# Two runs of eighteen W_out products instead of four runs of nine in the second MLP layer of an attention-and-MLP kernel

## The chip, the cores and the metric

The kernel runs on one core of one Trainium2 chip. The metric is the device time of one execution in microseconds (us). The kernel before takes 757.12 us, the median of three runs that lie between 756.71 and 757.83 us.

## What is computed

A clustered attention over two batches of 768 tokens with eight heads is followed by two MLP layers over all 1536 tokens (512 features, 2048 hidden features). Only the second MLP layer is touched by the change:

```python
def _moe2_ref(x, w_in, w_out):
    h = x @ w_in
    r = np.maximum(h, 0.0)
    g = r * r
    return (g @ w_out).astype(np.float32)
```

The first layer has the same shape with another activation. The weights come in as 64-bit floats, viewed as pairs of 32-bit words, and the kernel turns each 128-row or 128-column chunk into 32-bit floats on the way ("decode").

## The kernel before, in words

The two layers are worked off in 32 slots, numbered 0 to 31 here: layer, then batch, then a pair of hidden chunks (256 hidden features). Slots 16 to 23 are the second layer's first batch, slots 24 to 31 its second batch. A slot computes the hidden values of its pair (`h`, 256 features by 768 tokens) and applies the activation. The product with W_out belongs to the slot before: `second` returns a list `pend` of four closures, and each is a quarter of the W_out products of the previous slot, which are issued in between.

Every fp32 operand is held as a high and a low part (both fp32r), so each product is three matmuls: high by high, low by high, high by low.

From slot 8 on, the hidden values are formed from seven block products instead of eight, which accumulate in two PSUM banks, A and B. `product` issues 6 matmuls of 384 columns. Products 1, 3, 5 and 7 go to A, and products 2, 4 and 6 to B. Between them A and B are read while they hold partial sums: ScalarE copies A after product 1 and after product 3 and B after product 4 (lines 1123, 1139, 1142), and VectorE adds B after product 2, A after product 5 and B after product 6 (`total`). Product 7 is read by `active` (Relu on ScalarE, line 828). Product 5 accumulates in the bank that the copy after product 3 reads, and product 6 in the one that the copy after product 4 reads. The next slot swaps the banks, so its product 2 starts afresh in the bank that held product 7.

`active` squares twice on ScalarE, once rounded to fp32r (`gh`, line 831) and once in fp32 (line 832), and `low` subtracts the two on VectorE (`gl`, line 835). The left half of the first chunk (LO) is ready after product 2, the second chunk after product 6, and the right half of the first chunk (HI) after product 7.

In the second layer a quarter of `pend` is 9 matmuls of 512 columns (line 854): three token blocks by three terms. A slot has 36 of them and 42 matmuls in block products. The quarters stand behind products 2, 4, 6 and 7.

Work for later slots is spread over ScalarE and VectorE by hand. `early` and `late` split the next weights (lines 929 and 930: a cast on ScalarE, a subtraction on VectorE). `sums` forms weight sums on VectorE. `absolute` and `do` decode chunks for later: line 87 takes absolute values on ScalarE, lines 96, 98, 101 and 104 follow on VectorE one after the other, and step 4 stores a W_in chunk to DRAM or splits a W_out chunk (cast at line 110 on ScalarE, subtraction at 111 on VectorE). `COUNTS` gives two decode tasks to most slots, three to slot 17, one to slot 23, and none from slot 24 on. At a batch's end (`last`, slot 23) the five calls `nxt.part` split the next batch's inputs (cast at line 902, subtraction at 903); `rest`, the loop at line 1136, splits the last two in slots 16 and 24.

ScalarE, VectorE, TensorE and SyncE's DMA issues each stand in the order in which the code was written.

Of the kernel before, what the change touches and what calls it, by code (L numbers as in the profile page):

```python
# [35 lines left out]
def tile_kernel(ctx, tc, q, k, v, cent, w_in1, w_out1, w_in2, w_out2, cw_cols, out):  # L36
# [768 lines left out]
    LO, HI, ALL = slice(0, QB), slice(QB, S), slice(0, S)  # L805
# [9 lines left out]
    def total(layer, c, at, ps):  # L815

        dst = h[:, c, at]
        if layer == 0:
            nc.vector.tensor_tensor(out=dst, in0=ps, in1=dst, op=ALU.add)
        else:  # L820
            nc.vector._custom_dve(TENSOR_ADD_SAT, out=dst, in0=ps, in1=dst, s0=TOP, s1=0.0)  # L821
# [12 lines left out]
    def low(g, c, at):  # L834
        nc.vector.tensor_sub(g[1][:, at], h[:, c, at], f32(g[0][:, at]))  # L835
# [120 lines left out]
    def product(ps, w, wi, x, start=False):  # L956
        terms = [(0, 0), (0, 1), (1, 0)]
        for j, (a, z) in enumerate(terms):
            for kc in range(2):
                nc.tensor.matmul(ps, w[a][:, wi, kc * P:(kc + 1) * P], x[z][kc],  # L960
                                 start=start and j == kc == 0, stop=j == 2 and kc == 1, skip_group_check=True)
# [23 lines left out]
    def absolute():  # L985
        n = len(ready)
        if n < len(tasks) and n < len(fetched) and 5 * n <= len(steps) + 5:
            layer, kind, fc = tasks[n]
            if layer:
                if q < NP:  # L990
                    return
                t = rooms[n % 2]
            elif kind:
                t = room
                if 5 * n > len(steps) and tasks[n - 1][:2] != (0, 0):
                    return
            else:
                t = weights[fc // 2].chunk(fc)
            ready.append(magnitude(fetched[n], t.bitcast(U32)))
# [29 lines left out]
    slots = [(layer, b, p) for layer in range(2) for b in range(B) for p in range(NP)]  # L1029
    nxt = None  # L1030
    at_bank = 0
    ends = None
    for q, (layer, b, p) in enumerate(slots):
        bank = first if q == 0 else [
            duo.tile([P, QB], F32, tag=("sd", "pt0")[(at_bank + i) % 2], name="ps") for i in range(2)]
        A, B_ = bank
        n = COUNTS[q] if q < len(COUNTS) else 0
        more = q + 1 < len(slots)
        last = p == NP - 1 and more
        if p == 0:  # L1040
            combos = nxt
        if p == (3 if q >= NP else 1) and q < 3 * NP:
            nxt = Combos(slots[q + NP][1])
        wq = weights.get(q)
        ga, gb = g_tiles(), g_tiles()

        def before(k):
            if pend:
                pend[k]()
            if p == 0 and ends:  # L1050
                finish(*ends, k)

        def do(i, ks):
            if i < n:
                for k in ks:
                    step(k)

        if q + 2 < 2 * NP and q in PLAIN and q or q >= 2 * NP - 1 and more:
            at = q + 1 + (q in PLAIN)
            weights[at] = Weights(slots[at][0], slots[at][2], at >= NP)  # L1060
        wn = weights.get(q + 1)
        if q == 0:
            pend = None
            ends = None
            y = y_tiles()
            bank = [first, [hidden(xs, second_w, i, y[4 + i][:, 0:QB]) for i in range(2)]]
            for c, g in ((0, ga), (1, gb)):
                for i, at in enumerate((LO, HI)):
                    active(0, g, c, at, bank[c][i])
                if not c:  # L1070
                    absolute()
                for i, at in enumerate((LO, HI)):
                    low(g, c, at)
                if not c:
                    step(0)
                    step(1)
                    step(2)
                    step(3)
            wn.plain(1)
            step(4)  # L1080
            absolute()
            for k in range(4):
                step(k)
            absolute()
            step(4)
        elif q in PLAIN:
            extra = list(EXTRA.get(q, ()))
            for c, g in ((0, ga), (1, gb)):
                for i, at in enumerate((LO, HI)):
                    u = 2 * c + i  # L1090
                    bank[i] = hidden(xs, wq.sides[c], i, bank[i] if not c else None)
                    active(0, g, c, at, bank[i])
                    if u:
                        do(u - 1, (4,))
                    if i:
                        if q + 1 in PLAIN:
                            wn.plain(c)
                        else:
                            wn.early(c)
                    absolute()  # L1100
                    do(u, (0, 1))
                    low(g, c, at)
                    do(u, (2, 3))
                    if i:
                        before(2 * c)
                        before(2 * c + 1)
                    if i and not c and q + 1 not in PLAIN:
                        wn.sums()
                    if u == 3:
                        do(u, (4,))  # L1110
                    if extra:
                        kind, j = extra.pop(0)
                        (nxt.part if kind else nxt.sum)(j)
        else:
            at_bank = 1 - at_bank
            x = combos.tiles
            if p == 0:
                rooms = [t3_p.tile([P, S], F32, tag="t3", name="room")[:, 0:DM] for _ in range(2)]
            product(A, wq.x, wq.B11, x[Combos.A11], True)
            wq.late()  # L1120
            if q + 2 < 2 * NP:
                weights[q + 2] = Weights(slots[q + 2][0], slots[q + 2][2], q + 2 >= NP)
            nc.scalar.copy(h[:, 0, LO], A)
            if n:
                absolute()
            product(B_, wq.x, wq.B21, x[Combos.A12], True)
            total(layer, 0, LO, B_)
            active(layer, ga, 0, LO)
            do(0, (0, 1))
            if last:  # L1130
                nxt.part(0)
            do(0, (2, 3))
            low(ga, 0, LO)
            before(0)
            if p == 0:
                while len(x) < 7:
                    combos.part(len(x))
            product(A, wq.x, wq.T2, x[Combos.S2])
            nc.scalar.copy(h[:, 1, LO], A)
            do(0, (4,))  # L1140
            product(B_, wq.x, wq.T1, x[Combos.S1], True)
            nc.scalar.copy(h[:, 1, HI], B_)
            if more:
                wn.early(0)
            if last:
                nxt.part(1)
                nxt.part(2)
            if n > 1:
                absolute()
            before(1)  # L1150
            do(1, (0, 1))
            if n > 2:
                do(1, (2, 3))
            product(A, wq.y, wq.T3, x[Combos.S3])
            total(layer, 1, HI, A)
            product(B_, wq.y, wq.B22, x[Combos.S4])
            total(layer, 1, LO, B_)
            active(layer, gb, 1, ALL)
            if n > 2:
                do(1, (4,))  # L1160
                absolute()
            if more:
                wn.sums()
            end = min(n - 1, 2)
            if n > 2:
                do(2, (0, 1))
            if n > 1:
                do(end, (2,))
            low(gb, 1, ALL)
            if last:  # L1170
                nxt.part(3)
            before(2)
            product(A, wq.y, wq.T4, x[Combos.A22])
            active(layer, ga, 0, HI, A)
            if more and n < 2:
                wn.early(1)
            if n > 1:
                do(end, (3,))
            low(ga, 0, HI)
            if more and n > 1:  # L1180
                wn.early(1)
            if n > 1:
                do(end, (4,))
            if q < 3 * NP and 2 < p < 7:
                nxt.sum(p - 3)
            if last:
                nxt.part(4)
            before(3)

        if p == 0 and q:  # L1190
            y = y_tiles()
        pend = second(layer, y, [(g, 2 * p + i) for i, g in enumerate((ga, gb))],
                      None if p == NP - 1 else (0, 1) if q in PLAIN else (1, 0))
        ends = (layer, y, b)
    for k in range(4):
        pend[k]()
        finish(*ends, k, last=True)
# [34 lines left out]
```

## Time and profile before

| | us |
|---|---|
| median of three runs | 757.12 |
| span of the profiled execution, first to last instruction | 755.5 |
| TensorE busy | 749.0 (99%) |
| VectorE busy | 594.6 (79%) |
| ScalarE busy | 507.3 (67%) |

The profile does not give a time of the profiled execution beyond its span; the median lies 1.6 us above the span, which is what lies around it. "Busy" for TensorE counts overlapping matmuls, so its 99% says that it hardly ever stands still, not that it works at its peak. The trace gives every instruction's start, duration and what ended the idle time before it.

### The profile page before, as it was taken

The page shows a single profiled execution, that of the slowest core. Times are in us where ns is not written, and L with a number is a line of the kernel's source. Part 1 is how long each engine was busy: PE and PEld are TensorE (multiplying, and loading weights), DVE is VectorE, ACT ScalarE, POOL GpSimd, SP SyncE. Part 2 cuts the span into 40 slices and gives each one's busy share as a digit, 9 for nine tenths or more (in the row PEclk, how much of TensorE's full clock was granted, in tenths as well). Part 3 has the DMA queues.
Part 4 walks back from the last instruction along what each step waited for, and adds up shares of the span by engine and source line. Part 5 has one row for each costly group of instructions (what it writes and reads, how often), then busy time and mean ns, then how long its engine had stood idle before and what let it go on. Part 6 is the DMA issues. An engine that isn't in the chain of part 4 may idle for free.

```text
span 755.5 us, 12127 instructions
## 1 busy us (share of the span) xinstructions
PE 749.0 (99%) x4345; PEld 685.8 (91%) x4345; DVE 594.6 (79%) x1079; ACT 507.3 (67%) x1049; POOL 163.1 (22%) x221
## 2 busy tenths in 40 slices
PE   8999999999999999999999999999999999999998
PEld 5999999999999999999999999998898988989886
DVE  7999999989897888887988877898878886445432
ACT  7999999999898654544765554685656666455442
POOL 5848668568554100000000000000000000000000
PEclk9999999999999999999999999999999999999999
DMA  8796685573320745545444342323532203000002
GB/s 212 180 199 154 162 183 124 136 182 75 80 57 14 228 140 175 163 150 179 143 154 139 126 126 85 112 80 123 161 112 85 83 29 140 29 28 29 29 1 83
DMA packets 71900, 88.54 MB, mean 117 GB/s; under 512 B 30272, under 2 KB 53984, under 8 KB 71840
## 3 DMA queue, kind: packets, MB, share of 16 engines
q1 hardware_dynamic: 71296, 87.64, 41.1%
q8 instruction: 34, 0.56, 0.3%
q14 instruction: 26, 0.21, 0.1%
q10 hardware_dynamic: 544, 0.13, 0.1%
HBM read 58.76 MB, written 11.58 MB: 93 GB/s over the span
## 4 chain that ended last, share of the span: by engine, by line
PE 95%; DVE 2%; DMA 1%; ACT 1%; issue 0%; POOL 0%; ACTq 0%; DVEq 0%; POOLq 0%
PE ps L960 23%; PE y L854 17%; PE y L848 11%; PE pa L531 8%; PE pt L506 8%; PE y L850 6%; PE ps L482 4%; PE ps L484 4%; PE ph L139 4%; PE ps L139 3%; PE ps L335 1%; PE pt L272 1%; DMA raw<-in_moe_w_in_dram 1%; PE pm L361 1%; PE pz L181 1%; PE ps L345 0%
## 5 line engine op out<-in xcount | busy, mean ns | idle before, releaser
L831 ACT ACTIVATE gh<-h 128x384 fp32r<-128x384 f32 (+1 forms) x64 | 41.5, 648 | 101.3 <-DVE h L821 71.5
L519 DVE TENSOR_TENSOR el<-pt,eh 128x384 fp32r<-128x384 f32 x192 | 97.6, 550 | 7.0 <-ACT eh L516 6.4
L488 DVE TENSOR_REDUCE nm<-ps 128x1 f32<-128x768 f32 x96 | 91.5, 954 | 13.7 <-PE ps L484 12.6
L497 ACT ACTIVATE e<-ps,nm 128x768 f32<-128x768 f32 x96 | 87.9, 916 | 3.1 <-DVE nm L488 2.2
L516 ACT CAST eh<-pt 128x384 fp32r<-128x384 f32 x192 | 83.3, 490 | 7.6 <-PE pt L506 6.4
L835 DVE TENSOR_TENSOR gl<-h,gh 128x384 fp32r<-128x384 f32 (+1 forms) x104 | 67.2, 646 | 18.9 <-ACT h L832 18.7
L506 PE MATMUL pt<-identF,e 128*128 128x128 f32 x576 | 80.1, 274 | 0.1
L854 PE MATMUL y<-oh,gl 128*128 128x512 f32 x192 | 76.0, 396 | 0.0
L854 PE MATMUL y<-ol,gh 128*128 128x512 f32 x192 | 75.8, 395 | 0.0
L854 PE MATMUL y<-oh,gh 128*128 128x512 f32 x192 | 74.6, 389 | 0.0
L482 PE MATMUL ps<-k,q 128*128 128x512 f32 x192 | 69.1, 363 | 0.4 <-ACT e L497 0.4
L506 PEld LDWEIGHTS pt<-identF,e 128*128 128x128 f32 x576 | 65.4, 140 | 2.3 <-DVE el L519 1.4
L484 PE MATMUL ps<-k,q 80*128 80x512 f32 x192 | 60.9, 341 | 0.0
L930 DVE TENSOR_TENSOR wxl<-wb,wxh 128x512 fp32r<-128x512 f32 x37 | 25.6, 691 | 40.9 <-ACT wxh L929 40.8
L848 PE MATMUL y<-gh,ol 128*128 128x512 f32 x128 | 50.0, 391 | 0.0
L848 PE MATMUL y<-gh,oh 128*128 128x512 f32 x128 | 50.0, 391 | 0.0
L848 PE MATMUL y<-gl,oh 128*128 128x512 f32 x128 | 50.0, 391 | 0.0
L960 PE MATMUL ps<-xl,wxh 128*128 128x384 f32 x192 | 49.2, 337 | 0.0
L960 PE MATMUL ps<-xh,wxh 128*128 128x384 f32 x192 | 48.9, 335 | 0.1
L960 PE MATMUL ps<-xh,wxl 128*128 128x384 f32 x192 | 49.0, 336 | 0.0
L531 PE MATMUL pa<-eh,v 128*128 128x384 f32 x192 | 47.3, 361 | 0.0
L531 PE MATMUL pa<-el,v 128*128 128x384 f32 x192 | 46.7, 352 | 0.0
(226 smaller groups left out, 1902.8 us busy)
## 6 DMA issues: line engine op xcount, KB each, us to landing
raw<-in_moe_w_in_dram SPq DMA_DIRECT2D x32, 512.0 KB, 4.2
raw<-in_moe_w_out_dram SPq DMA_DIRECT2D x32, 512.0 KB, 3.6
wb<-wst SPq DMA_DIRECT2D x24, 512.0 KB, 4.1
q<-k SPq DMA_DIRECT2D x15, 384.0 KB, 4.6
wst<-room SPq DMA_DIRECT2D x16, 256.0 KB, 2.4
wst<-wb SPq DMA_DIRECT2D x13, 256.0 KB, 2.3
k<-k SPq DMA_DIRECT2D x16, 192.0 KB, 2.7
rawv<-in_v_dram SPq DMA_DIRECT2D x8, 384.0 KB, 6.1
```

Source lines behind the costliest of these rows:

```text
L482: nc.tensor.matmul(ps[:, a:a + n], q2[:, qs], k2[:, a:a + n], start=True, stop=False)
L484: nc.tensor.matmul(ps[:, a:a + n], q1[0:K1, qs], k1[0:K1, a:a + n], start=False, stop=True)
L488: nc.vector.tensor_reduce(out=nm, in_=live["s", t][:, 0:S], op=ALU.max, axis=AX, negate=True)
L497: nc.scalar.activation(e, live["s", t][:, 0:S], ACTF.Exp, bias=live.pop(("nm", t)), accum_out=sums[:, s:s + 1])
L506: nc.tensor.transpose(pt[:, i], e[:, kc * P:(kc + 1) * P], identF)
L516: nc.scalar.copy(place("eh", t, u), live["pt", t, u])
L519: nc.vector.tensor_tensor(out=place("el", t, u), in0=live.pop(("pt", t, u)), in1=f32(place("eh", t, u)), op=ALU.subtract)
L531: nc.tensor.matmul(pa, v2[:, i % NJ, :], src[:, i % NJ, :], start=(i == 0), stop=(i == 2 * NJ - 1))
L835: nc.vector.tensor_sub(g[1][:, at], h[:, c, at], f32(g[0][:, at]))
L848: nc.tensor.matmul(y[m], l[:, cs], r[:, 0:512], start=first, stop=last)
L854: nc.tensor.matmul(y[m], l[:, m * P:(m + 1) * P], r, start=(begin and z == 0), stop=(fc == KF - 1 and z == 2))
L960: nc.tensor.matmul(ps, w[a][:, wi, kc * P:(kc + 1) * P], x[z][kc], start=start and j == kc == 0, stop=j == 2 and kc == 1, skip_group_check ...
```

## The change

In the second layer, that is slots 16 to 31 (`long`), the previous slot's W_out products are issued as two runs of 18 behind products 2 and 6, instead of four runs of 9 behind products 2, 4, 6 and 7. With them several pieces of ScalarE's and VectorE's work change places:

- the first steps of a slot's first decode task stand ahead of the `total` of product 2 on VectorE;
- the split of a decoded W_out chunk (`do(0, (4,))`), the next absolute value and, in slot 23, input part 1 stand ahead of product 3 and its copy;
- the cast of the next weights' first half (`early(0)`) stays behind the copy of product 4;
- the second half (`early(1)`), input parts 2 to 4 and a second W_out split stand ahead of product 7 and its Relu;
- the last subtraction of a slot (`low` of the first chunk's HI half) is put off to the next slot (`owed`);
- the output copies of a finished batch (`finish`) stand behind the second run.

```diff
+            long = layer == 1
             product(B_, wq.x, wq.B21, x[Combos.A12], True)
+            if long:
+                do(0, (0, 1))
+                if owed:
+                    owed.pop()()
+                for k in range(2):
+                    pend[k]()
             total(layer, 0, LO, B_)
             active(layer, ga, 0, LO)
-            do(0, (0, 1))
+            if not long:
+                do(0, (0, 1))
             if last:
                 nxt.part(0)
             do(0, (2, 3))
             low(ga, 0, LO)
-            before(0)
-            if p == 0:
-                while len(x) < 7:
-                    combos.part(len(x))
+            if long:
+                rest()
+                do(0, (4,))
+                if last:
+                    nxt.part(1)
+                if n > 1:
+                    absolute()
+                do(1, (0, 1))
+                if n > 2:
+                    do(1, (2, 3))
+            else:
+                before(0)
+                rest()
             product(A, wq.x, wq.T2, x[Combos.S2])
             nc.scalar.copy(h[:, 1, LO], A)
-            do(0, (4,))
+            if not long:
+                do(0, (4,))
             product(B_, wq.x, wq.T1, x[Combos.S1], True)
             nc.scalar.copy(h[:, 1, HI], B_)
             if more:
                 wn.early(0)
...
             product(A, wq.y, wq.T3, x[Combos.S3])
+            product(B_, wq.y, wq.B22, x[Combos.S4])
+            if long:
+                for k in range(2, 4):
+                    pend[k]()
             total(layer, 1, HI, A)
-            product(B_, wq.y, wq.B22, x[Combos.S4])
             total(layer, 1, LO, B_)
             active(layer, gb, 1, ALL)
...
             low(gb, 1, ALL)
             if last:
+                if long:
+                    nxt.part(2)
                 nxt.part(3)
...
-            if more and n < 2:
+            if more and (n < 2 or long):
                 wn.early(1)
...
+                product(A, wq.y, wq.T4, x[Combos.A22])
+                active(layer, ga, 0, HI, A)
+                owed.append(lambda g=ga: low(g, 0, HI))
```

TensorE, slot 23, from product 4 (bank B, `ps_7411`) to the end of the nine W_out products behind it. Before:

```order
L960 MATMUL ps_7411<-xh_6360,wxh_7336 128x384 x2
L960 MATMUL ps_7411<-xl_6361,wxh_7336 128x384 x2
L960 MATMUL ps_7411<-xh_6360,wxl_7337 128x384 x2
L854 MATMUL y3_6568<-oh_7325,gh_7277 128x512
L854 MATMUL y3_6568<-ol_7326,gh_7277 128x512
L854 MATMUL y3_6568<-oh_7325,gl_7278 128x512
L854 MATMUL y4_6569<-oh_7325,gh_7277 128x512
L854 MATMUL y4_6569<-ol_7326,gh_7277 128x512
L854 MATMUL y4_6569<-oh_7325,gl_7278 128x512
L854 MATMUL y5_6570<-oh_7325,gh_7277 128x512
L854 MATMUL y5_6570<-ol_7326,gh_7277 128x512
L854 MATMUL y5_6570<-oh_7325,gl_7278 128x512
```

The same place now, products 3, 4, 5 and 6 (7409 is bank A, 7410 bank B):

```order
L960 MATMUL ps_7409<-xh_6323,wxh_7348 128x384 x2
L960 MATMUL ps_7409<-xl_6324,wxh_7348 128x384 x2
L960 MATMUL ps_7409<-xh_6323,wxl_7349 128x384 x2
L960 MATMUL ps_7410<-xh_6360,wxh_7348 128x384 x2
L960 MATMUL ps_7410<-xl_6361,wxh_7348 128x384 x2
L960 MATMUL ps_7410<-xh_6360,wxl_7349 128x384 x2
L960 MATMUL ps_7409<-xh_6387,wyh_7423 128x384 x2
L960 MATMUL ps_7409<-xl_6388,wyh_7423 128x384 x2
L960 MATMUL ps_7409<-xh_6387,wyl_7424 128x384 x2
L960 MATMUL ps_7410<-xh_6465,wyh_7423 128x384 x2
L960 MATMUL ps_7410<-xl_6466,wyh_7423 128x384 x2
L960 MATMUL ps_7410<-xh_6465,wyl_7424 128x384 x2
```

Product 5 now follows product 4 directly, where nine W_out products stood between them.

ScalarE, slot 22, from the squares of the first chunk's LO half to the next weights' first cast. Before:

```order
L831 ACTIVATE gh_7275<-h_3961 128x384
L832 ACTIVATE h_3961<-h_3961 128x384
L1139 COPY h_3961<-ps_7273 128x384
L110 CAST oh_7325<-room_6411 128x512
L1142 COPY h_3961<-ps_7274 128x384
L929 CAST wxh_7336<-wb_7279 128x512
L87 ACTIVATE room_6412<-raw64_7167 128x512
```

And now (lines 1162 and 1166 are the copies of products 3 and 4):

```order
L831 ACTIVATE gh_7274<-h_3961 128x384
L832 ACTIVATE h_3961<-h_3961 128x384
L110 CAST oh_7327<-room_6411 128x512
L87 ACTIVATE room_6412<-raw64_7185 128x512
L1162 COPY h_3961<-ps_7272 128x384
L1166 COPY h_3961<-ps_7273 128x384
L929 CAST wxh_7348<-wb_7278 128x512
```

The W_out cast and the next absolute value moved ahead of the copy of product 3.

ScalarE, slot 23, before (`xh` of `x1` are the casts of the next batch's inputs):

```order
L831 ACTIVATE gh_7412<-h_3961 128x384
L832 ACTIVATE h_3961<-h_3961 128x384
L902 CAST xh_7443<-x1_1_86 128x768
L1139 COPY h_3961<-ps_7410 128x384
L110 CAST oh_7466<-room_6411 128x512
L1142 COPY h_3961<-ps_7411 128x384
L929 CAST wxh_7477<-wb_7416 128x512
```

And now:

```order
L831 ACTIVATE gh_7411<-h_3961 128x384
L832 ACTIVATE h_3961<-h_3961 128x384
L902 CAST xh_7461<-x1_1_86 128x768
L110 CAST oh_7468<-room_6411 128x512
L902 CAST xh_7472<-x1_1_86 128x768
L1162 COPY h_3961<-ps_7409 128x384
L1166 COPY h_3961<-ps_7410 128x384
```

Here the W_out cast and a second input cast moved ahead of the copy of product 3.

VectorE, slot 23, from the subtractions of the slot's own weights to the end of its decode. Before:

```order
L930 TENSOR_TENSOR wyl_7425<-wb_7279,wyh_7424 128x256
L821 ISA h_3961<-ps_7411,h_3961 128x384
L96 TENSOR_SCALAR room_6411<-room_6411 128x512
L98 TENSOR_SCALAR room_6411<-room_6411 128x512
L903 TENSOR_TENSOR xl_7444<-x1_1_86,xh_7443 128x768
L101 SCALAR_TENSOR_TENSOR room_6411<-raw64_7254,room_6411 128x512
L104 SCALAR_TENSOR_TENSOR room_6411<-raw64_7254,room_6411 128x512
```

And now:

```order
L930 TENSOR_TENSOR wyl_7424<-wb_7278,wyh_7423 128x256
L96 TENSOR_SCALAR room_6411<-room_6411 128x512
L98 TENSOR_SCALAR room_6411<-room_6411 128x512
L835 TENSOR_TENSOR gl_7275<-h_3961,gh_7274 128x384
L821 ISA h_3961<-ps_7410,h_3961 128x384
L903 TENSOR_TENSOR xl_7462<-x1_1_86,xh_7461 128x768
L101 SCALAR_TENSOR_TENSOR room_6411<-raw64_7256,room_6411 128x512
L104 SCALAR_TENSOR_TENSOR room_6411<-raw64_7256,room_6411 128x512
```

The `total` of product 2 (L821) moved behind the first two decode steps and behind the put-off subtraction (L835). The DMA issues on SyncE keep their order.

## Rows read from the trace of the kernel before

**Rows 1.** The page, part 1: busy time, share of the span, instructions.

```profile
PE 749.0 (99%) x4345; PEld 685.8 (91%) x4345; DVE 594.6 (79%) x1079; ACT 507.3 (67%) x1049; POOL 163.1 (22%) x221
```

**Rows 2.** Cores: span and mean granted TensorE clock.

```profile
core 0: 755.5 us, clock 1.000
```

**Rows 3.** Chain that ended last: start us, duration us, what (xcount).

```profile
390.50 2.08 PE ps L960 x12
...
509.06 2.08 PE y L854 x9
511.14 2.10 PE ps L960 x12
...
522.66 2.12 PE ps L960 x12
...
538.91 2.10 PE ps L960 x12
...
554.62 2.10 PE ps L960 x12
...
601.74 2.10 PE ps L960 x12
...
617.65 2.10 PE ps L960 x12
...
633.74 2.10 PE ps L960 x12
```

**Rows 4.** Timeline of TensorE, last run: start, duration, engine, line, operation.

```profile
741.44 0.39 PE L854 MATMUL y<-oh,gh 128*128 128x512 f32 x1
...
743.52 0.39 PE L854 MATMUL y<-oh,gh 128*128 128x512 f32 x1
...
751.46 0.39 PE L854 MATMUL y<-oh,gl 128*128 128x512 f32 x1
```

**Rows 5.** Timeline of TensorE, product 5 of slot 24, with its idle time.

```profile
626.13 0.30 PEld L960 LDWEIGHTS ps<-xh,wyh 128*128 128x128 f32 x2 [0.48 <-ACT h L1139]
626.13 0.62 PE L960 MATMUL ps<-xh,wyh 128*128 128x384 f32 x2
...
626.59 0.51 PE L960 MATMUL ps<-xl,wyh 128*128 128x384 f32 x2
```

**Rows 6.** Timeline of ScalarE, end of slot 22 and slot 23.

```profile
599.69 0.49 ACT L828 ACTIVATE h<-ps 128x384 f32<-128x384 f32 x1 [0.82 <-PE ps L960]
600.22 0.53 ACT L831 ACTIVATE gh<-h 128x384 fp32r<-128x384 f32 x1
...
601.21 0.60 ACT L929 CAST wxh<-wt 128x512 fp32r<-128x512 f32 x1
...
602.76 0.40 ACT L929 CAST wyh<-wb 128x256 fp32r<-128x256 f32 x1
603.07 0.47 ACT L1123 COPY h<-ps 128x384 f32<-128x384 f32 x1
603.44 0.67 ACT L87 ACTIVATE room<-raw 128x512 f32<-128x512 f32 x1
...
606.44 0.82 ACT L902 CAST xh<-x 128x768 fp32r<-128x768 f32 x1
607.16 0.47 ACT L1139 COPY h<-ps 128x384 f32<-128x384 f32 x1
609.61 0.63 ACT L110 CAST oh<-room 128x512 fp32r<-128x512 f32 x1 [1.98 <-DVE room L104]
```

**Rows 7.** Timeline of VectorE, slot 23.

```profile
604.86 0.55 DVE L821 CUSTOM_DVE_ANT_0 h<-ps,h 128x384 f32<-128x384 f32 x1
605.33 0.42 DVE L96 TENSOR_SCALAR room<-room 128x512 f32<-128x512 f32 x1
...
608.16 0.68 DVE L101 SCALAR_TENSOR_TENSOR room<-raw,room 128x512 uint32<-128x512 uint32 x1
608.88 0.69 DVE L104 SCALAR_TENSOR_TENSOR room<-raw,room 128x512 uint32<-128x512 uint32 x1
```

More of the change, by code (lines that the diff above doesn't have):

```diff
@@ L1031, in tile_kernel @@
     at_bank = 0
+    owed = []
     ends = None
@@ L1116, in tile_kernel, with rest @@
             x = combos.tiles
+            long = layer == 1
             if p == 0:
                 rooms = [t3_p.tile([P, S], F32, tag="t3", name="room")[:, 0:DM] for _ in range(2)]
+            def rest():
+                while p == 0 and len(x) < 7:
+                    combos.part(len(x))
             product(A, wq.x, wq.B11, x[Combos.A11], True)
@@ L1144, in tile_kernel @@
                 wn.early(0)
[L1145 to L1153, printed above, removed]
+            if not long:
+                if last:
+                    nxt.part(1)
+                    nxt.part(2)
+                if n > 1:
+                    absolute()
+                before(1)
+                do(1, (0, 1))
+                if n > 2:
+                    do(1, (2, 3))
             product(A, wq.y, wq.T3, x[Combos.S3])
+            product(B_, wq.y, wq.B22, x[Combos.S4])
+            if long:
+                for k in range(2, 4):
+                    pend[k]()
             total(layer, 1, HI, A)
-            product(B_, wq.y, wq.B22, x[Combos.S4])
             total(layer, 1, LO, B_)
             active(layer, gb, 1, ALL)
+            if long and p == 0:
+                finish(*ends, 0)
+                finish(*ends, 1)
             if n > 2:
@@ L1170, in tile_kernel @@
             if last:
+                if long:
+                    nxt.part(2)
                 nxt.part(3)
-            before(2)
-            product(A, wq.y, wq.T4, x[Combos.A22])
-            active(layer, ga, 0, HI, A)
-            if more and n < 2:
+            if not long:
+                before(2)
+                product(A, wq.y, wq.T4, x[Combos.A22])
+                active(layer, ga, 0, HI, A)
+            if more and (n < 2 or long):
                 wn.early(1)
@@ L1178, in tile_kernel @@
                 do(end, (3,))
-            low(ga, 0, HI)
-            if more and n > 1:
-                wn.early(1)
+            if not long:
+                low(ga, 0, HI)
+                if more and n > 1:
+                    wn.early(1)
             if n > 1:
@@ L1187, in tile_kernel @@
                 nxt.part(4)
-            before(3)
+            if not long:
+                before(3)
+            else:
+                if p == 0:
+                    finish(*ends, 2)
+                    finish(*ends, 3)
+                product(A, wq.y, wq.T4, x[Combos.A22])
+                active(layer, ga, 0, HI, A)
+                owed.append(lambda g=ga: low(g, 0, HI))
         if p == 0 and q:
@@ L1194, in tile_kernel @@
         ends = (layer, y, b)
+    owed.pop()()
     for k in range(4):
```

## Prediction

> **What bounds the kernel now.** I read the busy shares first. TensorE is busy for 749.0 of 755.5 us and its granted clock is 1.000, the upper of its two levels (2.4 GHz) [rows 1, 2]. So it is the bound, and a change can only act through the spacing of its matmuls or through the few places where it waits. The second view is the chain that ended last. In the second layer it is TensorE almost without a break: 12 block-product matmuls in 2.10 us, 9 W_out products in 2.08, and so on, with one slot to the next in 554.62 - 538.91 = 15.71 us [rows 3]. Two things can be read from it.
>
> First, runs cost something where they start. In the first layer 12 block matmuls take 2.08 us, in the second, behind W_out products, 2.10 [rows 3]. The last run of W_out products starts at 741.44; its first nine take 743.52 - 741.44 = 2.08, and the 35 after them (751.46 - 743.52) / 35 = 0.227 each, so nine would take 2.04 [rows 4]. Each W_out run pays 0.04 at its start, each block run 0.02. The period says the same: 42 x 2.08 / 12 + 36 x 0.227 = 15.45, and 15.71 is 0.26 more, which four pairs of starts share at 0.065 each.
>
> Second, only three slots are longer: 522.66 to 538.91 is 16.25 (slot 18, 0.54 too long), 601.74 to 617.65 is 15.91 (slot 23, 0.20) and 617.65 to 633.74 is 16.09 (slot 24, 0.38) [rows 3]. That is 1.12 us. The wait in slot 24 shows the weak point: product 5 stood until ScalarE's copy of product 3 was done (the idle 0.48 before its weight load), and then its first two matmuls took 0.62, 0.11 over the usual 0.51 [rows 5].
>
> **The change part by part.** Nothing is removed; the same instructions stand in another order. I count from a slot's start 0, the end of the previous product 7, and add to the median, since no time of the profiled execution besides its span is shown; the 1.6 us around the span stay.
>
> *Fewer run starts.* From slot 17 to the end there were 15 x 4 = 60 starts of W_out runs (the flush at the end continues the last one), now 15 x 2 + 1 = 31. 29 pairs go, at 0.065: -1.9 us. It could be 29 x 0.02 = -0.6 if only the block side saves.
>
> Here stands a rule against the change. The Trainium skill, "TensorE: Matmul & The Clock Gate", Back-to-back issue gap, spaces matmuls by their columns and a constant and has no term for a run's start. By it this part gives 0, and the sum below would be 1.9 us higher; the rows show the term, and I go by them.
>
> *The old waits.* The three of 1.12 us come from places that are rearranged, so I take them out and price the new order from scratch: -1.1 us.
>
> *Less cover for the copies.* Product 5 now starts directly behind product 4. With products 1 and 2 (2.08), 18 W_out products (2.08 + 2.04) and products 3 and 4 (2.10) it is due at 8.30, and product 3 ends at 7.26. ScalarE's Relu started 0.19 after product 7 in the trace (599.69, where 599.50 was its end by the 0.19 that a read of PSUM follows later; an estimate). The copy can so run from 7.45 to 7.92: 0.4 to spare, in a slot where ScalarE is free. Product 6 behind the copy of product 4 and the next slot's product 2 behind the Relu have as much. In slots 25 to 31 nothing else stands there: no wait, 0 us, and if the margin failed, 0.11 to 0.5 each.
>
> *What stands ahead of the copy in slots 17, 19, 21 and 22.* Their first task is a W_out chunk. Relu 0.19, the first square 0.53 later, the next cast 1.52 later at 1.71 [rows 6]. Then (the other casts have moved ahead of the Relu) the two casts of `late` (0.52 from one to the next, as three stood between 601.21 and 602.76), 0.31 after the second the copy of product 1 at 2.54, the absolute value 0.37 later, 2.91 to 3.58 [rows 6]. VectorE waits for it: line 96 at 3.62, line 98 at 4.07 (0.42 each [rows 7] and a gap, an estimate), the put-off subtraction at 4.54 and the `total` at 5.01 (0.47 apart as 604.86 and 605.33), line 101 at 5.48, line 104 0.72 later, 6.20 to 6.89 [rows 7]. ScalarE waited for line 104 in the trace and followed 0.04 later (609.61) [rows 6]; now that wait stands ahead of the copy: cast 6.93, absolute value 0.52 later at 7.45, copy 8.0 to 8.5, product 5 at 8.57 instead of 8.30, and 0.11 for the restart: 0.38. In some of them a second W_out cast delays the Relu by 0.1 or VectorE comes late from a slot before. I take 0.45 each: +1.8 us. Ends: 0, and 1.0 each.
>
> *Slots 16 and 18.* In slot 16 two input casts and an absolute value stand ahead of the copy, with a decode that VectorE starts earlier: I take +0.2. Slot 17 decodes three chunks, and VectorE leaves it late: that was the 0.54 of slot 18. Now the `total` of product 6 in slot 17 stands behind four decode steps and ends some 0.4 later, so the second chunk's `gl` comes about 0.6 after the W_out products need it in slot 18; the copy of product 3 is late there by 0.3; and the W_out cast that now stands ahead of slot 18's Relu waits for a late line 104 and holds the next slot's product 2 by 0.5. Together +1.5 us, an estimate next to the 0.54; ends 0.5 and 2.5.
>
> *Slot 23* carries the largest term. Here the input casts join in, and everything up to the copy is one string. The `total` ends at 5.56 (as above), the two squares follow at 5.60 and 6.15, the input cast at 6.6 to 7.4 (0.82 [rows 6]). VectorE's line 101 started 0.90 after that cast's end in the trace (606.44 + 0.82 = 607.26, 608.16), line 104 0.72 later for 0.69 [rows 6, 7]: 8.3, 9.0 to 9.7. The W_out cast can begin at 9.75, the second input cast 0.52 later at 10.3, and the copy 0.72 behind it (606.44 to 607.16 [rows 6]), 11.0 to 11.5. Before, the copy stood ahead of that W_out cast, at 607.16, and the 1.98 us that ScalarE then waited for line 104 [rows 6] held only the copy of product 4. Now product 5 starts at 11.5 instead of 8.30, and with 0.11 for the restart and 0.1 that the slot before passes on it is +3.4 us. Ends: the 0.48 of [rows 5] and 4.2.
>
> In the trace ScalarE and VectorE have slack behind it, so by the same counting slot 24's two input casts are done by 7.0 and its copy is not late. SyncE's and GpSimd's queues keep their order; transfers that hang on a decode step move with it, and slot 18's weights are the only ones that come close.
>
> *Sum.* -1.9 - 1.1 + 1.8 + 0.2 + 1.5 + 3.4 = +3.9 us, 757.1 + 3.9 = 761.0 us.
>
> **The rivals.**
>
> *The clock falls.* TensorE stands for 3.2 us in slot 23. The rows hold no such pause, and the clock in them never left the upper level [rows 2]. If it fell to 1.2 GHz, products 5 and 6 would take 2.08 us more, and if part of the run behind them is slow too, up to 4. I take 763.1 us. For it: a long pause is new; against: only one, and the engine has been busy throughout before it. The same page of the Trainium skill, section "Why this matters for your kernels", warns of idle gaps between bursts for this reason; no row of the kernel before can show it.
>
> *No gain from longer runs.* The cost of a run's start might be a cost per W_out product wherever they stand between block products, since the 35 fast ones are the flush, with nothing else on TensorE. Then the W_out side saves little: 761.0 + 1.2 to 1.9 = 762.5 us. Against it: the block runs are back at the first layer's pace after their first six matmuls, so it looks like a passing state.
>
> *Not slower: the copy isn't late.* Everything hangs on when ScalarE reaches the copy of product 3. The margin in slots 17, 19, 21 and 22 is missed by 0.3 only. If line 104 ends by 6.6 instead of 6.9, and the squares and steps of slots 16 and 18 likewise come earlier, their 3.5 us go: 757.5 us, no change. If the string in slot 23 is cut as well, because part of it runs beside the rest, the wait there goes below 1 us: 755 us. For it: small margins, and ScalarE has 33% idle; against: the string in slot 23 is made of true dependences and the order of one queue.
>
> **How the numbers follow.** The forecast has 0.62, own range 759.5 to 762.6 us; the fall of the clock 0.10; no gain from longer runs 0.10; copies not late 0.18. Of these 0.18, 0.07 are faster and 0.10 within 0.2% (1.5 us, about what a measurement of this kernel can tell from no change), the rest just above it. Slower by more than that: 0.83. The range goes from 758.4, a forecast in which half of the short waits fail to come, to 763.6, above the clock rival.
>
> **What would show it.** Right: in the chain, W_out runs of 18 in 4.12 us; in slot 23 a wait of about 3 us before product 5, released by ScalarE's copy (line 1162), with line 110 and two of line 902 ahead of it; waits of 0.2 to 0.6 at product 5 in slots 17, 19, 21 and 22; none from slot 25 on, with a period of 15.57. Wrong: 18 products in 4.16; a copy at line 1162 before 8.3 in slot 23; a granted clock below 1.000; waits in the late slots.

## The result and the profile after

The changed kernel takes 762.87 us (median of five runs, 761.22 to 763.77) against 757.12 before: 1.0073 of its time, 95% interval 1.006 to 1.0085. It is slower by 5.7 us, 1.9 more than forecast. That is inside the stated range (758.4 to 763.6), but 0.3 above the forecast's own (759.5 to 762.6).

Page of the changed kernel, part 1, busy time by engine; it answers to [rows 1]:

```profile
PE 749.6 (99%) x4345; PEld 686.4 (90%) x4345; DVE 593.0 (78%) x1079; ACT 506.2 (67%) x1049; POOL 163.5 (22%) x221
```

Its span and mean granted clock, which answer to [rows 2]:

```profile
core 0: 759.4 us, clock 0.997
```

The counts are those of before. The span is 3.9 us longer while TensorE's busy time grew by 0.6: it stands. And the mean clock is no longer 1.000.

The chain that ended last (start, duration, what), from slot 20 to slot 25; it answers to [rows 3]:

```profile
550.14 4.12 PE y L854 x18
554.27 3.14 PE ps L960 x18
...
561.53 4.18 PE ps L960 x24
...
579.22 2.38 PE ps L960 x12
...
611.43 0.70 DVE room L104
...
612.15 0.62 ACT oh L110
612.77 0.73 ACT xh L902
613.51 0.39 ACT h L1162
...
613.94 3.33 PE ps L960 x12
617.26 4.71 PE y L854 x18
621.97 3.14 PE ps L960 x18
625.11 4.12 PE y L854 x18
```

A run of 18 takes 4.12 us, where two of nine took 4.16 [rows 3]. Away from waits the chain stays on TensorE, as before. In slot 23 it leaves TensorE for ScalarE and VectorE and comes back at product 5; the twelve matmuls of products 5 and 6 then take 3.33, where they take 2.38 behind the short wait in slot 21, and the run behind them 4.71 instead of 4.12.

The weight loads that waited at products 5, 2 and the W_out run in slots 18 to 23 (start, duration, what, in brackets the idle time and what ended it); they answer to [rows 5]:

```profile
525.03 0.19 PEld L854 LDWEIGHTS y<-oh,gl 128*128 128x128 f32 x1 [0.68 <-DVE gl L835]
...
530.96 0.30 PEld L960 LDWEIGHTS ps<-xh,wyh 128*128 128x128 f32 x2 [0.21 <-ACT h L1162]
...
540.13 0.30 PEld L960 LDWEIGHTS ps<-xh,wxh 128*128 128x128 f32 x2 [0.89 <-ACT h L828]
...
547.78 0.30 PEld L960 LDWEIGHTS ps<-xh,wyh 128*128 128x128 f32 x2 [0.41 <-ACT h L1162]
...
579.22 0.30 PEld L960 LDWEIGHTS ps<-xh,wyh 128*128 128x128 f32 x2 [0.33 <-ACT h L1162]
...
613.93 0.30 PEld L960 LDWEIGHTS ps<-xh,wyh 128*128 128x128 f32 x2 [3.31 <-ACT h L1162]
```

L1162 is now the copy of product 3, which stands ahead of product 5 in every slot of the second layer. ScalarE's timeline in slot 23 (answers to [rows 6]; the slot starts at 602.48) shows what stands ahead of the last one:

```profile
608.98 0.82 ACT L902 CAST xh<-x 128x768 fp32r<-128x768 f32 x1
612.15 0.62 ACT L110 CAST oh<-room 128x512 fp32r<-128x512 f32 x1 [2.36 <-DVE room L104]
612.68 0.83 ACT L902 CAST xh<-x 128x768 fp32r<-128x768 f32 x1
613.41 0.47 ACT L1162 COPY h<-ps 128x384 f32<-128x384 f32 x1
```

The copy could have run near 610; ScalarE stood 2.36 us for VectorE's line 104 instead. Busy times by window, product 5 and what follows it (the stretch, its length, busy time and instructions of PE, PEld, DVE, ACT and POOL, the granted clock, the DMA share and GB/s):

```profile
612.00:615.00 3.00, 1.06 (x6) 1.06 (x7) 2.42 (x5) 2.63 (x5) 0.00 (x0) 1.00 0.00 0
615.00:618.50 3.50, 3.50 (x12) 3.21 (x11) 2.15 (x5) 0.61 (x1) 0.00 (x0) 0.51 0.00 0
618.50:622.87 4.37, 4.37 (x22) 3.77 (x21) 4.04 (x8) 3.80 (x6) 0.00 (x0) 1.00 0.00 0
```

The granted clock is 0.51 from 615.0 to 618.5, so nearly all of that stretch ran at 1.2 GHz, behind a wait in which TensorE's matmuls had stood for 3 us.

How long each slot took, start to start, in us, worked out from the traces (slots 25 to 30 are alike in each kernel; e1 to e14 are the experiments below):

```
slot      16    17    18    19    20    21    22    23    24   25-30
before  15.60 15.68 16.25 15.71 15.71 15.71 15.71 15.91 16.09 15.71
after   15.75 15.80 16.35 16.81 15.57 15.88 15.85 20.39 15.57 15.57
e1      15.75 15.79 16.63 16.55 15.57 15.86 15.85 15.57 17.11 15.57
e2      15.60 15.67 19.81 16.28 15.57 16.29 16.87 16.89 17.20 15.57
e3      15.73 15.77 16.36 17.43 15.57 15.88 15.87 16.83 17.18 15.57
e4      15.60 15.68 16.26 15.71 15.71 15.71 15.71 15.91 15.60 15.57
e6      15.75 16.66 16.37 18.26 16.67 20.41 20.47 23.67 16.31 15.57
e7      15.60 15.83 19.28 16.86 16.09 17.47 17.47 19.74 16.29 15.57
e8      15.60 15.81 15.57 15.83 15.57 16.69 16.68 17.43 17.17 15.57
e9      15.60 15.57 19.49 15.57 15.57 15.59 15.59 17.51 16.65 15.57
e11     15.60 15.57 20.07 15.57 15.57 15.57 15.57 15.58 17.57 15.57
e13     15.60 15.57 17.05 16.09 15.57 15.57 15.57 18.00 15.60 15.57
e14     15.60 15.57 17.33 16.09 15.57 15.57 15.57 17.62 15.60 15.57
```

From slot 16 on the changed kernel loses 4.7 us. The gain is there too: 15.71 became 15.57.

### The profile page after: what moved, and what is told of

Its sections match the earlier page's. It is cut to its first block, busy times and chain, and to the rows that moved or that the text cites. A ratio compares the mean times of both kernels' runs of the same rounds, so it can differ in the third digit from the quotient of the medians.

```text
span 759.4 us, 12121 instructions
## 1 busy us (share of the span) xinstructions
PE 749.6 (99%) x4345; PEld 686.4 (90%) x4345; DVE 593.0 (78%) x1079; ACT 506.2 (67%) x1049; POOL 163.5 (22%) x221
## 4 chain that ended last, share of the span: by engine, by line
PE 91%; DVE 4%; ACT 3%; DMA 1%; issue 1%; POOL 0%; SPq 0%; POOLq 0%
PE ps L960 20%; PE y L854 14%; PE y L848 12%; PE pa L531 9%; PE pt L506 8%; PE y L850 6%; PE ps L482 4%; PE ph L139 4%; PE ps L484 4%; PE ps L139 4%; PE ps L335 1%; PE pt L272 1%; DMA wb<-wst 1%; PE pm L361 1%; PE y L139 1%
## 5 line engine op out<-in xcount | busy, mean ns | idle before, releaser
L835 DVE TENSOR_TENSOR gl<-h,gh 128x384 fp32r<-128x384 f32 (+1 forms) x104 | 67.0, 645 | 17.4 <-ACT h L832 17.1
```

## The experiments

Theory: longer runs save 0.13 us a slot, and the loss comes from ScalarE's and VectorE's work that now stands ahead of the copy of product 3, in slot 23 above all. Rivals: the longer runs lose by themselves; or the clock's fall is the main loss. All versions but e9 start from the changed kernel. Each ratio below is to the kernel before as it ran beside that version (medians 757.46 to 757.76 us).

**e4: the change in slots 24 to 31 alone.**

```diff
-            long = layer == 1
+            long = layer == 1 and b == 1
```

> The kernel before, with the two runs of 18 in slots 24 to 31 only, where no decode work is left. Theory (a run's start costs 0.065 per pair of starts): 15 of 32 starts go, -1.0, and slot 24's waits of 0.38 too: 755.6 to 756.0 us; a slot takes 15.57 instead of 15.71. Rival (the 40 ns at a W_out run's start are no start cost but the price of working between block products): 756.6 to 757.1, a slot 15.65 or more.

755.98 us, 0.9981 of before (0.9972 to 0.999): within the expected range, 0.2% faster, and the best version run. The chain from slot 23's last run of nine on:

```profile
615.67 2.08 PE y L854 x9
617.75 2.10 PE ps L960 x12
619.86 4.12 PE y L854 x18
623.98 4.18 PE ps L960 x24
628.16 4.12 PE y L854 x18
632.28 3.14 PE ps L960 x18
```

Without decoding beside it the change does what a run's start is worth, 18 products at 4.12, and nothing waits. The loss lies in slots 16 to 23.

**e1: in slot 23 the split and input part 1 behind product 4's copy.**

```diff
-                do(0, (4,))
-                if last:
-                    nxt.part(1)
+                if not last:
+                    do(0, (4,))
...
             if more:
                 wn.early(0)
+            if long and last:
+                do(0, (4,))
+                nxt.part(1)
```

> Changed kernel, but in slot 23 alone the split of the decoded W_out chunk and input part 1 stand behind the copy of product 4, as before the change. Theory (the string ahead of product 3's copy on ScalarE): product 5 of slot 23 no longer waits (3.15 us and 0.11 of restart go), TensorE's clock doesn't fall there (another 1.55 go), the late input part may hold the next slot's product 2 by up to 1.5: 758 to 759.5 us, granted clock 1.000. Rival (the two runs themselves take away the cover, whatever stands on ScalarE): a wait of over 2 us stays in slot 23 and the time stays above 761.

760.04 us, 1.0028 (1.0017 to 1.0039), 0.5 above the expected range. Slot 23 lost nothing (15.57 for 20.39), and the mean clock was 1.000. But 1.54 us came back in slot 24, at product 2:

```profile
621.87 0.61 PE L960 MATMUL ps<-xh,wxh 128*128 128x384 f32 x2 [1.24 <-ACT h L828]
```

The string ahead of the copy is the cause in slot 23, and with it the fall of the clock went too. What was taken from ahead of one copy stood ahead of the next reader, product 7's Relu (L828).

**e3: in slot 23 nine W_out products back between products 4 and 5.**

```diff
+            if long and last:
+                pend[2]()
             product(A, wq.y, wq.T3, x[Combos.S3])
...
-                for k in range(2, 4):
+                for k in range(3 if last else 2, 4):
```

> Changed kernel, but in slot 23 nine of the W_out products of the second run stand between products 4 and 5, so they fill 2.08 us of the wait; ScalarE's order is as changed. Theory (the pause lets the clock fall, which costs 1.55 in the profiled run and makes the times differ from run to run): the wait is 1.1, the granted clock stays 1.000, the time is 762.9 - 2.1 - 1.6 or lower, 758 to 759.3, and the runs lie within 1 us. Rival (the pause costs only itself): 760.8, with a spread as wide as the changed kernel's 2.5 us.

760.41 us, 1.0039 (1.0027 to 1.0052), 1.1 above the expected range. The cover of 2.08 us took the wait at product 5 from 3.31 to 1.3, with no fall of the clock, and the runs lie within 0.74 us. But TensorE now ended slot 23 3.6 us earlier, and ScalarE's Relu of product 7 came only 1.8 earlier: product 2 of slot 24 waited for it, and that slot lost 1.6. Half of the cover was not enough.

**e2: the e1 edit in all slots, the absolute value and the second chunk's first steps too.**

```diff
                 rest()
-                do(0, (4,))
-                if last:
-                    nxt.part(1)
-                if n > 1:
-                    absolute()
-                do(1, (0, 1))
...
                 wn.early(0)
+            if long:
+                do(0, (4,))
+                if last:
+                    nxt.part(1)
+                if n > 1:
+                    absolute()
+                do(1, (0, 1))
...
```

> Changed kernel, but in all sixteen slots of the second layer the split of the first decoded chunk, the next absolute value, the second chunk's first steps and input part 1 stand behind the copy of product 4. Theory: besides slot 23 the waits at product 5 in slots 16, 17, 21 and 22 (0.15 to 0.31 each) and about half of those in 18 and 19 go: 1 to 1.5 us below the kernel with slot 23 alone, 756.5 to 758.5. Rival (lost cover): the short waits stay, as in the kernel with slot 23 alone.

766.48 us, 1.0122 (1.0106 to 1.0137): the expectation failed by 9 us. No product 5 waits any more; product 2 waits for the Relu in six slots. The first and the last of them:

```profile
525.24 0.61 PE L960 MATMUL ps<-xh,wxh 128*128 128x384 f32 x2 [2.12 <-ACT h L828]
...
626.18 0.61 PE L960 MATMUL ps<-xh,wxh 128*128 128x384 f32 x2 [1.35 <-ACT h L828]
```

I had priced the copy's wait alone. In two runs of 18 a slot has two uncovered readings, the copies ahead of products 5 and 6 and the Relu ahead of the next product 2, and work moved from the first stands ahead of the second.

**e6, e7, e8: the Relu ahead of the second half of the next weights.** e6 puts `early(1)`, the last decode steps, the next sum and input part 4 behind product 7's Relu; e7 adds e2's edit; e8 also decodes two chunks in slot 17 (a third in slot 12 of the first layer instead), forms the sum of product 2 ahead of the first decode steps and moves the input parts further back.

```diff
...
                 active(layer, ga, 0, HI, A)
+                if more:
+                    wn.early(1)
+                if n > 1:
+                    do(end, (3,))
+                    do(end, (4,))
...
```

> Changed kernel, but the second cast of the next weights, the second W_out split and input part 4 stand behind product 7's Relu and squares, as before the change; ScalarE's order ahead of product 3's copy is as changed. Theory (two short covers, product 5 behind the copy of product 3 and product 2 behind the Relu; ScalarE's work moved from one shows at the other): the waits at product 2 in slot 19 go (0.8), but the slot's casts, copy and absolute value come 0.5 to 1.0 later, so the waits at product 5 in slots 17, 19, 21, 22 and 23 grow by as much: 765 to 767 us. Rival (each wait belongs to its own place): 762.0, with the waits at product 5 as in the changed kernel.

> Changed kernel with both: the first chunk's split and what followed it behind the copy of product 4, and the second cast, second split and input part 4 behind product 7's Relu. Theory (two short covers): hardly any wait at product 5, at product 2 only where VectorE or the input parts come late (slots 18, 23 and 24, together 1 to 3 us); the longer runs pay 1.9 and the old waits of 1.1 are gone: 755.5 to 757.5 us, granted clock 1.000. Rival (the two runs take away the cover): waits of 0.3 and more in most slots 16 to 23, 759 and above.

> As the kernel with both orders mended, and besides: slot 17's third decode task goes to slot 12 in the first layer, the total of product 2 stands ahead of the decode steps again, input part 1 stands behind the totals and parts 3 and 4 behind product 7's Relu. Theory: all slots of the second layer take 15.57 to 15.7, slot 12 stays at 15.60: 757.5 - 1.9 - 1.1 = 754.5, between 754.0 and 755.3 us, below both kernels. Rival (VectorE has no room left for these orders): waits of 1 us and more move to other slots, 755.5 to 757.

779.12 us (1.0283, 1.0269 to 1.0297), 768.94 (1.0145, 1.0129 to 1.016) and 762.92 (1.0067, 1.0055 to 1.008). e6 was worse than expected by 12 us or more, e7 and e8 missed by 11 and 8. In e6 the wait at product 5 grew to 1.91 in slot 21 and 4.91 in slot 23, product 4 there waited 1.51 for VectorE's sum of product 2, and the clock fell in slots 21, 22 and 23. VectorE's timeline in e8 shows what I had left out:

```profile
571.23 0.95 DVE L835 TENSOR_TENSOR gl<-h,gh 128x768 fp32r<-128x768 f32 x1
574.73 0.69 DVE L930 TENSOR_TENSOR wxl<-wt,wxh 128x512 fp32r<-128x512 f32 x1 [2.55 <-ACT wxh L929]
575.34 0.68 DVE L104 SCALAR_TENSOR_TENSOR room<-raw,room 128x512 uint32<-128x512 uint32 x1
576.71 0.69 DVE L111 TENSOR_TENSOR ol<-room,oh 128x512 fp32r<-128x512 f32 x1 [0.69 <-ACT oh L110]
```

The cast now waits for product 7 by way of the Relu, VectorE stands 2.55 us for its subtraction, line 104 behind it is late, and ScalarE's next split waits for that. So a wait on one of two queues that hand data to each other comes back on it by way of the other (2.55 on VectorE, then 1.36 on ScalarE). e8's slot 18 took 15.57, which fits that it pays for the third chunk of slot 17, though e8 moved other work as well; and the extra chunk cost 2.1 us in slot 13.

**e9: the kernel before with TensorE's order alone changed.**

```diff
...
+            if long:
+                for k in range(2):
+                    pend[k]()
             total(layer, 0, LO, B_)
...
             product(B_, wq.y, wq.B22, x[Combos.S4])
+            if long:
+                for k in range(2, 4):
+                    pend[k]()
...
```

> The kernel before with nothing but TensorE's order changed: two runs of 18 W_out products behind products 2 and 6 in slots 16 to 31, while ScalarE and VectorE keep the order of the kernel before (no first split, absolute value or input part ahead of the copy of product 3; product 7's Relu is read ahead of the next weights' second cast). Theory (what costs time in the changed kernel is the work put ahead of the copies, not the longer runs): from the kernel before, -2.0 for the run starts and -1.1 for its old waits; what hung on product 7's Relu comes about 2.0 us later against the slot's start, so ScalarE's copy of product 1 moves from 1.49 to 3.5 and VectorE's sum of product 2 from 3.3 to 5.3, and the copy of product 3 still stands near 7.5 in slots 17 and 19 to 22: no wait over 0.2 there and a period of 15.57 to 15.8. The first split between the two copies holds product 6 in slot 18 (about 1.3) and slot 23 (about 1.8), and slot 24 loses about 1.5 at product 5. Sum 757.7 - 3.1 + 4.6 = 759 us, 757 to 761. Rival (the runs themselves take the copies' cover away, whatever stands ahead of them): waits at products 5 or 6 in most of the slots 17 to 24, 762 us or more.

761.1 us, 1.0039 (1.0026 to 1.0052); the time came out 2 above the 759 expected, just above the range, by slot 18. In slots 17 and 19 to 22 nothing waits, though all are decoding, and the chain there stays on TensorE:

```profile
559.94 4.12 PE y L854 x18
564.07 4.18 PE ps L960 x24
568.25 4.12 PE y L854 x18
572.37 3.14 PE ps L960 x18
```

So in these slots the longer runs don't uncover the copies by themselves: the short waits of the changed kernel come from its new order on ScalarE and VectorE under the longer runs (the new order with runs of nine was not run). But slot 18 loses 3.9 us, more than in the changed kernel: its W_out run waits for `gl`, then runs slowly (granted clock 0.50 from 530 to 532). And slots 23 and 24 lose 1.9 and 1.1, where product 6 waits for the copy of product 4 (line 1146 here) and product 5 for that of product 3 (line 1143).

```profile
527.38 0.19 PEld L854 LDWEIGHTS y<-oh,gl 128*128 128x128 f32 x1 [2.28 <-DVE gl L835]
...
615.61 0.30 PEld L960 LDWEIGHTS ps<-xh,wyh 128*128 128x128 f32 x2 [1.97 <-ACT h L1146]
631.23 0.30 PEld L960 LDWEIGHTS ps<-xh,wyh 128*128 128x128 f32 x2 [1.12 <-ACT h L1143]
```

**e11: e9's order (and the split behind product 4's copy) in slots 16 to 23, the new order from 24.**

```diff
-            long = layer == 1
+            long = layer == 1 and b == 1
+            mid = layer == 1 and b == 0
...
+            if mid:
+                do(0, (4,))
...
```

> Slots 16 to 23: TensorE's two runs of 18 with ScalarE's and VectorE's order of the kernel before, except that a slot's first split stands behind the copy of product 4 as well; slots 24 to 31: as in the changed kernel. Theory: no wait over 0.3 in slots 16 to 23 but in slot 18, since no split stands ahead of either copy; slot 24 loses up to 1.5, slots 25 to 31 nothing (15.573 each). 757.7 - 2.0 - 1.1 + 0.5 (slots 18 and 23) + 1.5 = 756.6 us, 755 to 757.5, faster than the kernel before and near the version with the change in slots 24 to 31 alone. Rival (what is taken from ahead of one wait turns up at the next, as when all splits were moved): waits of 0.5 to 1.5 at product 2 or 4 in slots 17 to 23, 760 us or more.

760.76 us, 1.0035 (1.0023 to 1.0046): missed by 4, the range ended at 757.5. Slots 17 and 19 to 23 are free of waits (slot 23: 15.58); slot 18 loses 4.5 and slot 24 2.0. Busy times by window in slot 18 (columns as above):

```profile
526.00:528.00 2.00, 0.88 (x5) 0.44 (x3) 1.93 (x5) 2.00 (x6) 0.00 (x0) 1.00 0.00 0
528.00:530.00 2.00, 1.28 (x4) 1.09 (x5) 2.00 (x4) 0.43 (x1) 0.00 (x0) 0.81 0.00 0
530.00:532.00 2.00, 2.00 (x6) 1.51 (x6) 2.00 (x5) 0.22 (x1) 0.00 (x0) 0.50 0.96 240
```

VectorE is busy for all of it, TensorE is not, and then the clock falls.

**e13, e14: slot 18 mended.** Both form slot 17's `gl` ahead of its last split and decode steps; e13 leaves slot 23 as before, e14 gives it 18, 9 and 9 products behind products 2, 6 and 7.

```diff
...
+            if ahead:
+                low(gb, 1, ALL)
             if n > 2:
                 do(1, (4,))
                 absolute()
...
```

> The version that combined the two orders, with two edits: in slot 17, which decodes three chunks, the subtraction that gives gl of the second chunk stands ahead of the second chunk's split and the decode steps (VectorE stood 2.30 us idle there for the split's cast, and gl is ready when ScalarE's first square is), and slot 23 has runs of nine and the order of the kernel before. Theory: the 1.84 us wait for gl in slot 18 and the fall of the clock behind it go; what may stay there is up to 0.7 at product 5, because VectorE still leaves slot 17 late. Slot 23 as in the kernel before (15.91), slot 24 15.60. Against the kernel before: -0.1 (slot 17), -0.4 (18, +0 to -0.7), -0.54 (19 to 22), -0.5 (24), -0.9 (25 to 31): 757.7 - 2.3 = 755.4 us, 754.8 to 756.2. Rival (slot 18's loss is VectorE's lateness, not the place of that one subtraction): slot 18 still loses 2 us or more, 757.5 us or more.

> As the one before, except slot 23: 18 W_out products behind product 2, nine behind product 6, nine behind product 7, and its first split behind the copy of product 4. Theory: product 5 doesn't wait there (with two runs of 18 in this order slot 23 took 15.580), and nine products behind product 7 give its Relu the cover that slot 24 lacked (0.92 and 0.48 of waits): slot 23 at 15.64, slot 24 at 15.6 to 15.8. Against the version with nines in slot 23 that is -0.27 to -0.1: 755.2 us, 754.6 to 756.2. Rival (the new batch's input splits in slot 24 come late whatever covers product 7): slot 24 loses 1 us or more, 756.3 us or more.

758.82 us (1.0019, 1.001 to 1.0028) and 758.63 (1.0015, 1.0006 to 1.0024), 3.4 above what was expected of each. The wait for `gl` and the fall of the clock in slot 18 are gone; of its loss 1.5 and 1.8 stay, and slot 19 loses 0.5. The largest miss in e13 is slot 23: 18.00 where 15.91, the figure of the kernel before, was expected: products 4, 6 and 7 wait 0.89, 1.06 and 0.61 there. Its string starts 2.1 us later against the slot's start than there (Relu of product 7 at +0.2 instead of -1.9), because slot 22 no longer has nine W_out products behind product 7. e13's chain names the next thing that is late there, the weights read back from DRAM behind line 104 and a store:

```profile
527.38 0.70 DVE room L104
...
528.95 6.82 DMA wb<-wst
535.77 0.02 issue
535.80 0.63 ACT wxh L929
```

In slot 23 e14's product 7 waits 1.72 for VectorE's sum of product 5. In both, a change of order between two slots costs what the one had put off. Where these last microseconds could be saved is open; e4 remains ahead.

## Why the prediction was right, step by step

*Fewer run starts*, -1.9: the period went from 15.71 to 15.57 as forecast. 14 slots by 0.134 and 0.09 at the end are -2.0, and e4 shows it alone in slots 24 to 31. The rival without this gain falls. The rule of the Trainium skill ("TensorE: Matmul & The Clock Gate", "Back-to-back issue gap"), which has no term for a run's start, does not hold here: the trace's 0.134 us a slot decides. The run of 18 is 4.12, not 4.16, so the W_out side saves its part too.

*The old waits*, -1.1, went, at least from slot 24; what slot 18 has now is counted as new.

*The short waits*, 3.5 together: over 15.57 (15.60 in slot 16) there are 0.15 in slot 16, 0.23, 0.77, 1.24, 0.31 and 0.28 in slots 17, 18, 19, 21 and 22, together 3.0. For slot 18 three things were named: `gl` late by 0.6 (0.68), product 3's copy by 0.3 (0.21), the next product 2 held by 0.5 (0.89 at its weight load). That the copy waits for line 104 by way of the split held in slots 17, 19, 21 and 22, here in slot 21:

```profile
577.60 0.62 ACT L110 CAST oh<-room 128x512 fp32r<-128x512 f32 x1 [0.24 <-DVE room L104]
...
578.72 0.45 ACT L1162 COPY h<-ps 128x384 f32<-128x384 f32 x1
```

In slots 16 and 18 no split stands ahead of the copy. e9 confirms it from the other side in slots 17, 19, 21 and 22: without the new order these waits are gone.

*Slot 23*, +3.4: the copy was put at 11.0 to 11.5 after the slot's start and ran from 10.93 to 11.40. The slot took 4.82 more than 15.57. Of that the clock's fall has (3.33 - 2.37) + (4.71 - 4.12) = 1.55, 2.37 being products 5 and 6 behind a wait without a fall (2.36 and 2.38 in slots 19 and 21); the rest, 3.27, is the step as priced. e1 takes both away.

*The clock*: here the forecast was wrong. I gave its fall 0.10 and priced it at 2.1, and a clock below 1.000 was one of my signs of being wrong; it fell, for 3.4 us, and cost 1.55 in the profiled run. All five runs have mean clocks of 0.995 to 0.998. So what happened is forecast and rival together: -2.0 - 1.1 + 3.0 + 3.3 + 1.55 = +4.7, where the forecast had +3.9; without the clock +3.2. The rival's 763.1 is the nearest figure to the median, and the median lies in the stated range only because the range had been drawn to take in this rival: to that extent it was luck. The argument against it ("only one, and the engine has been busy throughout before it") counted for nothing. Its warning in the Trainium skill, "TensorE: Matmul & The Clock Gate", section "Why this matters for your kernels", agrees with this trace, where the clock fell behind a wait of 3.31.

The last microsecond between +4.7 and the medians' 5.7 isn't settled. The profiled run is the fastest of the five and reached slot 16 at 490.46, the kernel before at 491.22, by the same instructions (the versions whose first layer is unchanged lie between 490.64 and 492.20); and the run at 763.32 had a mean clock of 0.995, so its slow stretch may have been longer. Only one of the five was seen in a trace.

What I had not seen: neither order suits all slots. The new one is better than e9's in slots 18 and 24, and worse in 16, 17, 19, 21, 22 and 23. A reason shows in the busy times of the changed kernel, slots 16 to 24 and slots 25 to 30 (columns as above):

```profile
490.50:638.40 147.90, 144.00 (x716) 128.27 (x715) 118.75 (x220) 91.01 (x167) 0.00 (x0) 0.99 0.26 89
638.40:731.90 93.50, 93.50 (x471) 84.58 (x470) 43.60 (x86) 44.85 (x84) 0.00 (x0) 1.00 0.13 46
```

VectorE (third pair) is busy for 118.75 of 147.9 us while chunks are decoded, and for 43.6 of 93.5 after it. The mean of 78% over the span hides this. In the second stretch every order that was run takes the same 15.57 a slot with runs of 18; in the first, work moved from ahead of one reading of a bank showed at the next (e1, e2).

## What to carry to other kernels

Longer runs of one kind of product saved a fixed cost at each run's start here (0.134 us a slot), and they can take away the cover under the readings of partial sums between them: count both, and make such a change only where the other engines have room (here the slots without decoding, e4). Work moved away from ahead of one reading has to be priced at the next reading on the same queue, and where two in-order queues hand data to each other, at the other queue's next instruction as well. A pause of TensorE can cost more than its length (in slot 23 1.55 us on top of 3.27): check the granted clock of the stretch behind it.

## What the runs showed of the hardware that I had not expected

Pauses and the clock (waits as counted at the weight load). In slot 23 of the changed kernel the granted clock was at 1.2 GHz for 3.4 us behind a wait of 3.31. It also fell behind 2.44 (e2, slot 18) and behind 0.22 and 2.28 (e9, slot 18). It stayed at 1.00 behind 2.16 (e14, slot 23) and 1.97 (e9, slot 23), and also behind 1.62 and 2.29 in one slot (e7, slot 18). So the length of the waits alone doesn't tell in these traces whether the clock falls; what decides is open. Nor need it fall in every run of one kernel: four of e9's five runs have a mean clock of 0.998 and take 760.81 to 761.42 us, the fifth has 1.000 and takes 759.68.

The restart behind a wait costs slightly more than the 0.11 that I took: in slot 21 the first matmul of product 5 takes 0.62 instead of 0.51, and from its start to that of the W_out run behind product 6 it is 2.22 us, 2.08 in slot 20, where nothing waits. The chain's 2.36 and 2.38 against 2.10 overstate this: behind a wait it counts from the first matmul's start to the last one's end (2.38 for the 2.22), elsewhere from end to end, which leaves 0.16 out.
